# Fused bucketed attention and channel-mix kernel: transfers planned by DMA bandwidth, the second pair of heads turned by PE, v of four pairs left whole, and an early warm-up

## The chip, the cores and the metric

The kernel runs on one core of one Trainium2 chip. The metric is the device time of one execution in microseconds (us), lower is better. The profile's span (first to last instruction of the core) is about 2 us shorter than the time. An execution over 1.5% above the fastest of the same kernel counts as slow; ratios use the fast ones. A ratio is the mean time of one kernel's fast runs over that of the other's fast runs of the same rounds, so it is not quite the ratio of the medians that are quoted.

## The reference, cut to what matters

Attention in which a query sees only keys that fall in the same bucket (signs of six projections), then a channel mix on its result. The sizes are 4 batches, 8 heads, 768 positions, head dimension 64, model dimension 512, hidden dimension 1024, in float32.

```python
q_bits = (einsum('bhsd,dk->bhsk', q, proj) > 0)          # the same for k
mask   = bucket(q)[..., :, None] == bucket(k)[..., None, :]
scores = where(mask, (q @ k.T) / sqrt(D), -1e9)
attn   = softmax(scores) @ v                              # sum + 1e-9 below
x      = heads side by side                               # (B, S, 512)
x_prev = x shifted by one position
xk, xr = mu_k*x + (1-mu_k)*x_prev,  mu_r*x + (1-mu_r)*x_prev
out    = sigmoid(xr @ w_r) * (relu(xk @ w_k)**2 @ w_v)
```

The profile's names: a *pair* is two heads of one batch, so there are 16 pairs, four to a batch. The channel mix of a batch (called MoE in the program) can start only when all four of its pairs are finished and mixed.

## The kernel before

The program holds a small planner. Every operation is added with an engine, an estimated duration, a priority and its dependencies. A list scheduler then simulates all engines and fixes the order of instructions on each engine before the launch. On the chip each engine runs its list in that order, so one late operand holds everything behind it on that engine.

```python
LAG = {"PE": 0.35, "ACT": 0.30, "DVE": 0.30, "POOL": 0.30, "SP": 2.2, "GQ": 2.5}
# SP: transfers issued by SyncE; GQ: transfers issued by POOL. A transfer is
# done "lag" us after it was issued, however many others are in flight.
```

The parts that the change touches (cuts marked):

```python
# the projection, queued on ACT behind two k loads
for e in range(2):
    add("ACT", 0.06, -8.0, lambda e=e: nc.scalar.dma_start(out=pj[e * D : (e + 1) * D, :], in_=proj), w=[("pj", e)], lag=2.2)

# ten weight loads, each reading 512 KB of float32, from 10 us on
add("GQ", 1.1, 0.6 + 0.25 * i, f_w, w=[...], at=10.0 + 2.0 * i, lag=4.0)

def add_v(n):        # centre v: three POOL sums, a mean by matmul, two DVE ops
    ...              # vt, vs; mean: ones x vs; va = v - mean
def add_prep(n):     # q and k of a pair: hi and lo half-precision parts ...
    ...
    add("DVE", DVE_C(768, 2), n - 1.7, hi, ...)
    add("DVE", DVE_C(768), n - 1.7, lo, ...)
    # ... turned by a DMA transpose, one for q and one for k
    add("SP", 0.5, n - 1.5, tr, ..., lag=4.5, name=f"tr{n}")
    ...              # bits by PE and DVE, then four row copies by DMA:
    add("SP", 0.35, n - 0.7 + 0.01 * i, row, r=[("bx", sx, 0), ("bx", sx, 1)], w=[("ab", side, sa, j)])

def add_scores(n):   # nine steps of 1024 columns: PE scores, ACT exponential
    ...
def add_mix(n):      # xk = df*mu + x, in two DVE operations; the same for xr
    ...
```

Only pair 0 was turned by PE; pairs 1 to 15 by DMA.

The softmax here doesn't subtract the row's maximum and nothing guards it: scores larger than these inputs give would overflow.

Of the kernel before, what the change touches and what calls it, by code (L numbers as in the profile page):

```python
# [17 lines left out]
LAG = {"PE": 0.35, "ACT": 0.30, "DVE": 0.30, "POOL": 0.30, "SP": 2.2, "GQ": 2.5}  # L18
# [6 lines left out]
class Plan:  # L25
# [15 lines left out]
    def add(self, eng, dur, prio, fn, r=(), w=(), take=None, give=(), lag=None, name="", at=0.0):  # L41
        o = Op()
        o.i = len(self.ops)
        o.eng, o.dur, o.fn, o.prio, o.name = eng, dur, fn, prio, name
        o.take, o.give = take, give
        o.lag = LAG[eng] if lag is None else lag
        o.at = at
        deps = set()
        for key in r:
            if key in self.writer:  # L50
                deps.add(self.writer[key])
        for key in w:
            if key in self.writer:
                deps.add(self.writer[key])
            deps.update(self.readers.get(key, ()))
        for key in r:
            self.readers.setdefault(key, []).append(o.i)
        for key in w:
            self.writer[key] = o.i
            self.readers[key] = []  # L60
        o.deps = deps
        o.succ = []
        o.left = len(deps) + 1
        for d in deps:
            self.ops[d].succ.append(o.i)
        self.ops.append(o)
        return o

    def schedule(self):
# [17 lines left out]
        t = 0.0  # L87
        while len(order) < len(ops):
            while events and events[0][0] <= t + 1e-9:
                _, kind, i = heapq.heappop(events)  # L90
                if kind == 0:
                    met(i)
                elif kind == 1:
                    o = ops[i]
                    for s in o.succ:
                        if ops[s].eng == o.eng and o.eng not in ("SP", "GQ"):
                            met(s)
                else:
                    o = ops[i]
                    for s in o.succ:  # L100
                        if ops[s].eng != o.eng or o.eng in ("SP", "GQ"):
                            met(s)
                    for name in o.give:
                        cls, slot, moe = held.pop(name)
                        avail[cls].append(slot)
                        moe_held[cls] -= moe
            progress = False
            for e in free:
# [4 lines left out]
                while ready[e]:  # L113
                    item = heapq.heappop(ready[e])
                    o = ops[item[1]]
                    if o.take is not None:
                        cls, name, moe = o.take
                        if not avail[cls] or (moe and moe_held[cls] >= self.slots[cls][1]):
                            skipped.append(item)
                            continue  # L120
                    pick = o
# [15 lines left out]
                heapq.heappush(events, (t + o.dur, 1, o.i))  # L137
                heapq.heappush(events, (t + o.dur + o.lag, 2, o.i))
# [10 lines left out]
def kernel(  # L149
# [19 lines left out]
    P = 128  # L169
# [8 lines left out]

    QS = 4.0
# [12 lines left out]
    NQ, NNH, NAQ, NBX, NV, NVA, NPT, NOB, NRC = 3, 2, 3, 2, 3, 3, 2, 2, 4  # L192
# [6 lines left out]
    vt_t = [buf([P, 2, 3 * D], FP32, f"vt{i}") for i in range(1)]  # L199
    vs_t = [buf([P, 2, D], BF16, f"vs{i}") for i in range(NVS)]  # L200
    va_t = [buf([P, 2, NSC, D + 2], BF16, f"va{i}") for i in range(NVA)]
# [33 lines left out]
    ACT_C = lambda n: 0.093 + 0.833 * n / 1000.0  # L235
    MM = lambda n: n / 2400.0 + 0.0025
    POOL2 = lambda n: 0.08 + 2.2 * n / 1000.0


    def f_ids():  # L240
        nc.gpsimd.memset(idh, 0.0)
        nc.gpsimd.affine_select(
            out=idh, in_=idh, compare_op=ALU.not_equal, fill=1.0, base=0,
            pattern=[[-1, P]], channel_multiplier=1,
        )
# [5 lines left out]
    add("DVE", 0.08, -9.0, lambda: nc.vector.memset(p2, 0.0), w=["p2"])  # L251
    for i in range(NVA):
# [3 lines left out]
    for e in range(2):  # L256
        add("ACT", 0.06, -8.0, lambda e=e: nc.scalar.dma_start(out=pj[e * D : (e + 1) * D, :], in_=proj), w=[("pj", e)], lag=2.2)
# [6 lines left out]
    for t, src, key in ((muk, moe_mu_k, "muk"), (mur, moe_mu_r, "mur")):  # L264
# [3 lines left out]
        add("SP", 0.5, -0.5, f_mu, w=[key])  # L268
        add("DVE", 0.08, 0.5, lambda t=t: nc.vector.tensor_scalar(
# [4 lines left out]
    for i, (which, c0, n) in enumerate(wlist):  # L274
# [6 lines left out]
        add("GQ", 1.1, 0.6 + 0.25 * i, f_w, w=[("w" + which, c) for c in range(c0, c0 + n)], at=10.0 + 2.0 * i, lag=4.0)  # L281
# [4 lines left out]
    def add_load(n):  # L286
        b, t = divmod(n, NPB)
        s = n % NQ
        for side in "qk":
            if n == 0:  # L290
                for j in range(2):
                    def f(side=side, j=j):
# [3 lines left out]
                    add("SP" if side == "q" else "ACT", 0.4 if side == "q" else 0.06, -10.0 + j, f,  # L296
                        w=[("nat", side, s, j)], lag=2.6 + j * 0.5)
            else:
# [3 lines left out]
                add("SP", 0.4, n - 2.6, f, w=[("nat", side, s, j) for j in range(2)], lag=3.0)  # L302
# [4 lines left out]
        add("SP", 0.4, n - 2.3, fv, w=[("vn", n % NV)], lag=3.0)  # L307

    def add_v(n):
        s, sa, ss, sm_ = n % NV, n % NVA, n % NVS, n % NMC  # L310
        vn = vn_t[s].rearrange("p j (c d) -> p j c d", d=D)
        vt, vs = vt_t[0], vs_t[ss]

        def f1():
            nc.gpsimd.tensor_tensor(out=vt, in0=vn_t[s][:, :, 0 : 3 * D], in1=vn_t[s][:, :, 3 * D : 6 * D], op=ALU.add)  # L315

        def f2():
            nc.gpsimd.tensor_tensor(out=vt[:, :, 0:D], in0=vt[:, :, 0:D], in1=vt[:, :, D : 2 * D], op=ALU.add)

        def f3():  # L320
            nc.gpsimd.tensor_tensor(out=vs, in0=vt[:, :, 0:D], in1=vt[:, :, 2 * D : 3 * D], op=ALU.add)

        add("POOL", POOL2(384), n - 0.6, f1, r=[("vn", s)], w=["vt"], name=f"vsum{n}")
        add("POOL", POOL2(128), n - 0.6, f2, r=["vt"], w=["vt"])
        add("POOL", POOL2(128), n - 0.6, f3, r=["vt"], w=[("vs", ss)])
# [21 lines left out]
    def add_prep(n):  # L347
        s, sh, sa, sx = n % NQ, n % NNH, n % NAQ, n % NBX
        for side in "qk":
            nat, nh, a = side_nat[side][s], side_nh[side][sh], side_a[side][sa]  # L350
            def hi(side=side, nat=nat, nh=nh):
                nc.vector.tensor_scalar(out=nh[:, :, 0:D], in0=nat.rearrange("p j (c d) -> p (j c) d", d=D),
# [4 lines left out]
            def tr(side=side, nh=nh, a=a):  # L357
# [4 lines left out]
            add("DVE", DVE_C(768, 2), n - 1.7, hi, r=rn, w=[("nhh", side, sh)], name=f"hi{n}")  # L362
            add("DVE", DVE_C(768), n - 1.7, lo, r=rn + [("nhh", side, sh)], w=[("nhl", side, sh)], name=f"lo{n}")
            add("SP", 0.5, n - 1.5, tr, r=[("nhh", side, sh), ("nhl", side, sh)],
                w=ax + [("ab", side, sa, j) for j in range(2)], lag=4.5, name=f"tr{n}")
        for h in range(2):
# [16 lines left out]
            add("PE", 2 * MM(HALF) + 0.1, n - 0.8, f, r=["p1", "p2"] + [("a", side, sa, j) for side in "qk" for j in range(2)],  # L383
                w=[(nm,)], take=("sm", nm, 0), name=nm)
            add("DVE", DVE_C(HALF), n - 0.75, g, r=[(nm,)], w=[("bx", sx, h)], give=[nm], name=f"bx{n}")
        for i in (0, 1, 2, 3):
# [4 lines left out]
            add("SP", 0.35, n - 0.7 + 0.01 * i, row, r=[("bx", sx, 0), ("bx", sx, 1)], w=[("ab", side, sa, j)], name=f"row{n}")  # L391

    def add_prep_first(n):
        s, sh, sa = n % NQ, n % NNH, n % NAQ
        for j in range(2):
            pr = -8.0 + 2.0 * j
            for side in "qk":
# [17 lines left out]
                def ev(nm=nm, a=a, j=j, side=side):  # L415
                    i_ = sm(nm)[:, 0:HALF].bitcast(FP16)
                    if side == "q":
# [9 lines left out]
                add("DVE" if side == "q" else "ACT", DVE_C(768, 2) if side == "q" else ACT_C(768), pr, ev,  # L427
                    r=[(nm,)], w=[("a", side, sa, j), ("ab", side, sa, j)], give=[nm], name="ev" + nm)
            for side in "qk":
                for h in range(2):  # L430
# [6 lines left out]
                    def be(nm=nm, a=a, j=j, h=h):  # L437
# [3 lines left out]
                            scalar1=0x8000, scalar2=0x5400, op0=ALU.bitwise_and, op1=ALU.bitwise_or)  # L441
                    add("PE", 2 * MM(HALF) + 0.1, pr + 0.1, bits, r=["p1", "p2", ("a", side, sa, j)], w=[(nm,)], take=("sm", nm, 0), name=nm)
                    add("DVE", DVE_C(HALF), pr + 0.1, be, r=[(nm,)], w=[("ab", side, sa, j)], give=[nm], name="be" + nm)
# [31 lines left out]
    def add_pv(n):  # L475
        b, t = divmod(n, NPB)
        sp, sa, so = n % NPT, n % NVA, n % NOB
        for j in range(2):
# [3 lines left out]
            for g in range(3):  # L482
                def f(nm=nm, j=j, g=g):
                    oo = sm(nm)
                    for ic in (2 * g, 2 * g + 1):
                        for jc in range(NSC):
                            o = j * NSC * S + jc * S + ic * P
                            nc.tensor.matmul(oo[:, ic * 65 : ic * 65 + 65], pt_t[sp][:, o : o + P], va_t[sa][:, j, jc, 0 : D + 1],  # L488
                                             start=(ic == 0 and jc == 0), stop=(ic == NSC - 1 and jc == NSC - 1))
                add("PE", 12 * 0.0315, T + 0.02 * g, f, r=[("pt", sp, s) for s in steps] + [("va", sa, j), ("va1", sa)],  # L490
# [3 lines left out]
            def fd(nm=nm, sr=sr):  # L494
                oo = sm(nm)[:, 0:390].rearrange("p (c e) -> p c e", e=65)
                nc.vector.tensor_scalar(out=rc_t[sr][:, 0, :], in0=oo[:, :, D], scalar1=TINY, scalar2=None, op0=ALU.add)  # L496
# [6 lines left out]
            add("DVE", 2 * DVE_C(10), T + 0.1, fd, r=[(nm,)], w=[("rc", sr)], name=f"rc{n}")  # L503
# [9 lines left out]
        def fx(nm=nm):  # L513
            nc.vector.tensor_scalar(out=xt_t[sx][:, P:], in0=sm(nm)[:, 0:HALF].bitcast(BF16),  # L514
# [6 lines left out]
        add("DVE", DVE_C(768, 2) + 0.1, n + 1.45, fx, r=[(nm,), ("mc", smc)], w=[("xt", sx)], give=[nm], name=f"xt{n}")  # L521
        add("POOL", 0.25, n + 1.5, fs, r=[("xt", sx), ("xz", sx)], w=[("xs", sx)], name=f"xs{n}")

    def add_mix(n):
# [7 lines left out]
        for m, mu, dst in (("xk", muk, xk_t), ("xr", mur, xr_t)):  # L532
            def f1(mu=mu, dst=dst):
                nc.vector.tensor_scalar(out=dst[smx], in0=df_t[sd], scalar1=mu[:, t : t + 1], scalar2=None, op0=ALU.mult)

            def f2(dst=dst):
                nc.vector.tensor_tensor(out=dst[smx], in0=dst[smx], in1=x, op=ALU.add)
            pr = n + (1.65 if m == "xk" else 1.75)
            key = (m, smx)
            add("DVE", DVE_C(768, 4), pr, f1, r=[("df", sd), "mu" + m[1]], w=[key], name=f"{m}a{n}")  # L540
            add("DVE", DVE_C(768, 2), pr, f2, r=[key, ("xt", sx)], w=[key], name=f"{m}b{n}")

    def add_moe(b):
# [24 lines left out]
        for c in range(NSC):  # L568
# [28 lines left out]
            add("SP", 0.4, T + 0.35, st, r=[("os", so)], name=f"st{b}_{c}")  # L597
# [54 lines left out]
```

## Time and profile before

| | before |
|---|---|
| time, median of 3 | 289.43 us (288.86 to 290.68) |
| span of the profiled run | 290.1 us (its time 291.86 us, above the other three) |
| PE busy | 241.3 us (83%) |
| first exponential; first Relu of the channel mix | 18.1 us; 98.0 us |
| DMA share, 0 to 60 us | 1.03 of 16 engines |

First the page of the kernel before: its heading, and three rows of the second part, where the span is cut into 40 slices of 7.25 us and each digit is the busy share in tenths (for PEclk, the granted clock in tenths).

```profile
span 290.1 us, 6291 instructions
...
PE   0585412956968798999999999999999999999994
...
PEclk9999575895999999999999999999999999999998
DMA  7989999989387497374847370638270001111022
```

PE is often idle or half idle in the first 15 slices (109 us) and full after that. The early slices are also where DMA is full and where the granted clock falls to half. Busy times by stretch say it in numbers. The columns are: the stretch, its length, then busy us and instruction count of PE, PE weight loads, DVE, ACT and POOL, then clock, DMA share and GB/s. The two rows are the stretches that the prediction quotes.

```profile
17.00:113.00 96.00, 63.69 (x733) 37.05 (x732) 70.62 (x149) 56.34 (x65) 27.93 (x40) 0.86 0.90 195
113.00:286.00 173.00, 171.15 (x1703) 103.69 (x1720) 120.80 (x276) 123.36 (x168) 15.64 (x26) 1.00 0.40 99
```

```profile
0.00:60.00 60.00, 27.97 (x263) 15.70 (x264) 35.11 (x71) 20.14 (x22) 22.86 (x47) 0.83 1.03 221
60.00:110.00 50.00, 39.63 (x493) 23.56 (x491) 41.53 (x87) 37.39 (x44) 12.78 (x18) 0.93 0.75 194
110.00:290.00 180.00, 173.74 (x1719) 104.96 (x1733) 124.38 (x284) 126.09 (x173) 16.32 (x28) 1.00 0.39 98
```

The first 110 us are where time is lost: PE is busy 28.0 of 60, then 39.6 of 50 us. What PE waits for is in the chain of waits, the chain of work that ended last, followed back from the end. Each row has start, length and what filled it.

```profile
2.24 5.65 DMA pj<-in_proj_dram
...
21.52 10.16 DMA ak<-kh
...
32.51 5.68 DMA ak<-kh
...
42.30 6.71 DMA ak<-bx
...
60.82 4.32 DMA vn<-in_v_dram
...
80.99 3.79 DMA vn<-in_v_dram
```

The projection load (`pj`, 1.5 KB) opens the chain. Then come two DMA transposes (`ak<-kh` is k turned): 10.2 us and 5.7 us, where one at 99.6 us took 3.9 us. Then come the copies of pair 1's bucket bits into its turned tiles (`ak<-bx`). The bits were ready at 33.8 us, but SP issued these copies only from 41.3 us: in its list the rest of pair 2's transpose, one of pair 3 and three loads stand before them, and that one of pair 3 alone held SP for 4.4 us. So pair 1 waited for loaded transfers and for its place in SP's list. SP's timeline:

```profile
36.25 4.37 SPq L358 DMA_TRANSPOSE aq<-qh  x1
...
41.33 0.86 SPq L390 DMA_DIRECT2D aq<-bx  x1
```

From 60 us on, v loads are on the chain. ACT's timeline shows what pair 1's delay cost; in brackets is the idle time before the instruction and its releaser.

```profile
19.50 7.58 ACT L466 ACTIVATE pt<-sc 128x1024 bf16<-128x1024 f32 x8 [0.41 <-PE sc L462]
50.12 1.94 ACT L466 ACTIVATE pt<-sc 128x1024 bf16<-128x1024 f32 x2 [23.05 <-PE sc L462]
```

The first row ends pair 0 at 27 us; ACT then stands for 23 us.

### The profile page before, as it was taken

To read this page: it belongs to the slowest core of one execution; us is meant where nothing else is said; L and a number is where in the kernel's file an instruction comes from. 1 tells how busy PE (TensorE), PEld (TensorE's weight loads), DVE (VectorE), ACT (ScalarE), POOL (GpSimd) and SP (SyncE) were. 2 spreads that over 40 slices of the span, in tenths; PEclk is the share of its full clock that TensorE was granted. 3 is DMA by queue.
4 is the path that set the end of the run, shared out by engine and by line. 5 is a ranking of instruction groups with operands and counts; after the bars stand their busy time and mean duration, and the time that the engine had idled before them with its cause. 6 is when DMAs were issued, how large, how long until landed. Compare 5 with 4: busy or idle time off the path is not lost.

```text
span 290.1 us, 6291 instructions
## 1 busy us (share of the span) xinstructions
PE 241.3 (83%) x2470; PEld 144.2 (50%) x2488; DVE 201.0 (69%) x440; ACT 183.6 (63%) x237; POOL 52.0 (18%) x92
## 2 busy tenths in 40 slices
PE   0585412956968798999999999999999999999994
PEld 0333301531534565565656656565566666655441
DVE  0899440898697898979498989796677674476321
ACT  3247000873877787977677979676879887617420
POOL 2660324414231312300000303030200000000000
PEclk9999575895999999999999999999999999999998
DMA  7989999989387497374847370638270001111022
GB/s 228 314 197 153 263 199 215 236 180 278 82 233 161 130 252 161 79 187 129 210 146 161 99 145 29 129 114 187 92 129 23 4 7 50 61 72 40 28 82 107
DMA packets 67757, 40.55 MB, mean 140 GB/s; under 512 B 49960, under 2 KB 64144, under 8 KB 67728
## 3 DMA queue, kind: packets, MB, share of 16 engines
q1 hardware_dynamic: 65072, 37.14, 51.2%
q0 software_dynamic: 2208, 2.62, 6.4%
q8 instruction: 19, 0.31, 0.4%
q10 hardware_dynamic: 448, 0.40, 0.4%
q14 instruction: 10, 0.08, 0.1%
HBM read 24.12 MB, written 6.29 MB: 105 GB/s over the span
## 4 chain that ended last, share of the span: by engine, by line
PE 59%; DMA 17%; DVE 16%; POOL 2%; SPq 2%; issue 2%; ACTq 0%; ACT 0%; DVEq 0%; POOLq 0%
PE sc L462 14%; PE sm L585 13%; PE sm L556 10%; PE sm L488 8%; PE sm L575 6%; DMA ak<-kh 5%; DMA vn<-in_v_dram 4%; DMA ak<-bx 4%; PE sm L374 3%; DMA pj<-in_proj_dram 2%; PE sm L436 2%; DVE kh L355 1%; DMA aq<-qh 1%; PE sm L511 1%; SPq L358 1%
## 5 line engine op out<-in xcount | busy, mean ns | idle before, releaser
L466 ACT ACTIVATE pt<-sc 128x1024 bf16<-128x1024 f32 x144 | 143.5, 1028 | 63.7 <-PE sc L462 63.4
L462 PE MATMUL sc<-aq,ak 128*128 128x512 f16 (+1 forms) x384 | 86.4, 336 | 13.9 <-DMA ak<-bx 10.0
L462 PEld LDWEIGHTS <-ak 128*128 128x128 f16 x384 | 35.0, 99 | 44.8 <-issue 13.0
L556 PE MATMUL sm<-xk,wk 128*128 128x384 bf16 x256 | 48.4, 326 | 2.6 <-DVE ob L501 2.5
L488 PEld LDWEIGHTS <-pt 128*128 128x128 bf16 x1152 | 43.3, 98 | 10.5 <-issue 2.1
L585 PE MATMUL sm<-wv,k 128*128 128x512 bf16 x185 | 46.9, 379 | 0.5
L488 PE MATMUL sm<-va,pt 128*128 128x65 bf16 x1152 | 44.8, 195 | 0.7 <-DVE bx L378 0.7
L560 ACT ACTIVATE kr<-sm 128x384 bf16<-128x384 f32 x64 | 30.8, 496 | 8.7 <-PE sm L556 8.7
L556 PEld LDWEIGHTS <-wk 128*128 128x128 bf16 x256 | 24.0, 98 | 18.8 <-issue 4.4
L315 POOL TENSOR_TENSOR vt<-vn 128x384 f32<-128x384 f32 x16 | 18.3, 1141 | 78.5 <-DMA vn<-in_v_dram 78.5
L592 DVE SCALAR_TENSOR_TENSOR os<-rs,sm 128x512 f32<-128x512 f32 x24 | 16.4, 683 | 20.3 <-PE sm L585 19.2
L563 DVE TENSOR_TENSOR k<-kr 128x384 bf16<-128x384 bf16 x64 | 23.8, 383 | 7.1 <-ACT kr L560 7.0
L578 ACT ACTIVATE rs<-sm 128x512 f32<-128x512 f32 x24 | 14.4, 600 | 19.9 <-PE sm L575 15.2
L585 PEld LDWEIGHTS <-k 128*128 128x128 bf16 x192 | 18.1, 98 | 17.0
L518 POOL COPY xt<-xt 128x127 bf16<-128x127 bf16 x16 | 6.5, 408 | 103.9 <-DVE xt L514 103.9
L575 PE MATMUL sm<-wr,xr 128*128 128x512 bf16 x85 | 23.9, 379 | 0.5
L374 PE MATMUL sm<-ak,p 128*32 128x384 f16 x120 | 14.5, 354 | 7.3 <-DMA ak<-kh 7.3
L514 DVE TENSOR_SCALAR xt<-sm,mc 128x768 bf16<-128x768 bf16 x16 | 9.8, 612 | 15.2 <-PE sm L511 15.0
L496 DVE TENSOR_SCALAR rc<-sm 128x6 f32<-128x6 f32 x32 | 5.2, 162 | 20.6 <-PE sm L488 20.6
L378 DVE TENSOR_SCALAR bx<-sm 128x384 uint16<-128x384 uint16 x30 | 15.8, 549 | 5.2 <-PE sm L374 5.1
L501 DVE TENSOR_TENSOR ob<-sm,rc 128x384 bf16<-128x384 f32 x32 | 17.8, 557 | 1.1
L337 DVE SCALAR_TENSOR_TENSOR va<-sm,vn 128x384 bf16<-128x384 f32 x32 | 16.9, 549 | 0.8 <-PE sm L332 0.8
(58 smaller groups left out, 208.8 us busy)
## 6 DMA issues: line engine op xcount, KB each, us to landing
vn<-in_v_dram SPq DMA_DIRECT2D x16, 384.0 KB
out_dram<-os SPq DMA_DIRECT2D x24, 256.0 KB
qn<-in_q_dram SPq DMA_DIRECT2D x15, 384.0 KB
kn<-in_k_dram SPq DMA_DIRECT2D x15, 384.0 KB
wk<-in_moe_w_k_dram POOLq DMA_DIRECT2D x4, 256.0 KB, 7.2
wv<-in_moe_w_v_dram POOLq DMA_DIRECT2D x4, 256.0 KB, 5.3
wr<-in_moe_w_r_dram POOLq DMA_DIRECT2D x2, 256.0 KB, 7.7
aq<-bx SPq DMA_DIRECT2D x30, 9.0 KB
```

The costliest lines, as they stand in the source:

```text
L315: nc.gpsimd.tensor_tensor(out=vt, in0=vn_t[s][:, :, 0 : 3 * D], in1=vn_t[s][:, :, 3 * D : 6 * D], op=ALU.add)
L337: nc.vector.scalar_tensor_tensor(out=va_t[sa][:, j, :, 0:D], in0=sm(nm)[:, j * D : (j + 1) * D].unsqueeze(1).to_broadcast([P, NSC, D]), sc ...
L374: nc.tensor.matmul(ps[32 * i : 32 * i + 32, 0:HALF], w_, a[:, i // 2, h * HALF : (h + 1) * HALF], start=st, stop=not st)
L462: nc.tensor.matmul(ps[:, lo - s * STEP : hi - s * STEP], side_a["k"][sa][:, j, jc * P : (jc + 1) * P], side_a["q"][sa][:, j, q0 : q0 + hi ...
L466: nc.scalar.activation(out=pt_t[sp][:, s * STEP : (s + 1) * STEP], in_=sc_t[plan.slot[nm]], func=AF.Exp, bias=EBIAS, scale=ESC)
L488: nc.tensor.matmul(oo[:, ic * 65 : ic * 65 + 65], pt_t[sp][:, o : o + P], va_t[sa][:, j, jc, 0 : D + 1], start=(ic == 0 and jc == 0), stop ...
L501: nc.vector.tensor_tensor(out=ob_t[so][:, :, j * D : (j + 1) * D], in0=oo[:, :, 0:D], in1=rc_t[sr][:, 1, :].unsqueeze(2).to_broadcast([P, ...
L556: nc.tensor.matmul(ps[:, 0:HALF], wk_sb[:, d, fc * P : (fc + 1) * P], xk_t[mx[d]][:, h * HALF : (h + 1) * HALF], start=(d == 0), stop=(d = ...
L560: nc.scalar.activation(out=kr_t[sk], in_=sm(nm)[:, 0:HALF], func=AF.Relu, scale=0.5 ** 0.5)
L563: nc.vector.tensor_tensor(out=k2_t[s2][:, h * HALF : (h + 1) * HALF], in0=kr_t[sk], in1=kr_t[sk], op=ALU.mult)
L575: nc.tensor.matmul(sm(nr), xr_t[mx[d]][:, c * P : (c + 1) * P], wr_sb[:, d, :], start=(d == 0), stop=(d == NDC - 1))
L585: nc.tensor.matmul(sm(nv), k2_t[(b * NFC + fc) % NK2][:, c * P : (c + 1) * P], wv_sb[:, fc, :], start=(fc == 0), stop=(fc == NFC - 1))
```

## The change

The intent: let the planner know that transfers share a bandwidth, so that its order is one that the chip can keep, and take work off DMA and DVE in the first four pairs. The new limit (`BACKLOG`) acts only inside the plan: what the chip sees of it is another order in each engine's list. The core of the diff:

```diff
-LAG = {"PE": 0.35, "ACT": 0.30, "DVE": 0.30, "POOL": 0.30, "SP": 2.2, "GQ": 2.5}
+LAG = {"PE": 0.30, "ACT": 0.25, "DVE": 0.20, "POOL": 0.20, "SP": 1.8, "GQ": 2.0}
+BACKLOG = 1.5
 ...
+                    if o.svc > 0.3 and dma_free - t > BACKLOG:     # hold it back
+                        skipped.append(item)
+                        heapq.heappush(events, (dma_free - BACKLOG, 3, o.i))
+                        continue
 ...
+                if o.svc:                                          # one shared DMA server
+                    dma_free = max(t + o.dur + 0.9, dma_free) + o.svc
+                    lag = max(lag, dma_free + 0.6 - t - o.dur)
 ...
+    NWARM = 8
+    NPET = 1          # pairs up to this one are turned by PE
+    NUC = 4           # pairs whose v stays whole
+    POOL_HI = (1, 2)  # pairs whose hi is computed by POOL
-    NQ, NNH, NAQ, ... = 3, 2, 3, ...
+    NQ, NNH, NAQ, ... = 3, 2, 4, ...
 ...
+    for i in range(NWARM):   # dummy matmuls on zeros; an early Exp loads ACT's table
+        add("PE", 0.43, -20.0 + 0.1 * i, lambda: nc.tensor.matmul(sm("warm"), wz[:, 0:P], wz, ...), ...)
-        add("ACT", 0.06, -8.0, ... nc.scalar.dma_start(out=pj...), lag=2.2)
+        add("GQ", 0.6, -20.0, ... nc.gpsimd.dma_start(out=pj...), svc=0.05)
-        add("GQ", 1.1, 0.6 + 0.25 * i, f_w, ..., at=10.0 + 2.0 * i, lag=4.0)
+        add("GQ", 0.7, (2.2 + 0.5 * i) if which == "k" else (3.5 + 0.35 * i), f_w, ...,
+            at=(22.0 + 5 * i) if which == "k" else (34.0 + 3.5 * i), svc=1.5)
-            add("SP", 0.5, n - 1.5, tr, ..., lag=4.5)
+            if n <= NPET:    # 12 transposes a side by PE, two DVE copies a side
+                ...
+                continue
+            add("SP", 1.5, n - 1.8, tr, ..., svc=2.1)
+            # v of pairs 0 to 3: a POOL cast; the sum of v, times 1e-12, is added by one
+            # more matmul in PV, which also stands in for the mean of empty buckets
+                    if uc and g == 0:
+                        nc.tensor.matmul(oo..., tiny, vsu_t[n % NVS][:, j, :]... , start=True, stop=False)
-                nc.vector.tensor_scalar(out=dst[smx], in0=df_t[sd], scalar1=mu..., op0=ALU.mult)
-                nc.vector.tensor_tensor(out=dst[smx], in0=dst[smx], in1=x, op=ALU.add)
+                nc.vector.scalar_tensor_tensor(out=dst[smx], in0=df_t[sd], scalar=mu..., in1=x, op0=ALU.mult, op1=ALU.add)
```

Cut: some evictions of pair 0 moved from DVE to ACT, earlier priorities for preparing a pair, later loads of the mixing factors, and planned durations. Pairs 2 to 15 are still turned by DMA.

## The prediction

> **What bounds the kernel now.** The table of stretches shows two regimes. From 113 to 286 us PE is busy 171 of 173 us, clock 1.00, DMA share 0.40: bound by PE. From 17 to 113 us PE is busy 63.7 of 96 us, mean clock 0.86, DMA share 0.90: it waits.
>
> - The chain of waits opens with the projection load, 5.65 us, queued on ACT behind other loads; DVE idles 7.1 us for it (waits view). First scores: 17.4 us.
> - Pair 1's DMA transposes (10.2, then 5.7 us) and row copies (6.7 us) stand in the chain from 21.5 to 49 us. ACT idles 23 us between pairs 0 and 1, PE idles from 40 to 48 us, the clock falls to 0.5.
> - From 60 to 97 us attention takes 10 to 12 us a pair, though nine exponentials need 9.25 us (1028 ns each); v loads, POOL sums and DVE are on the chain.
>
> The MoE needs four finished pairs: its first Relu is at 98 us.
>
> **What the change does.**
>
> - Start: projection first on POOL's queue, early table load, PE warm-up. The Trainium skill, "Trainium Kernel Development and Optimization", Key Constraints, says that SP, ACT and POOL transfers share 16 DMA engines and interleave; the trace agrees (1.5 KB took 5.65 us at DMA share 0.75). The first k half had landed by 4.2 us: DVE can start 4 us earlier. Eight bit matmuls took 2.72 us, four later ones 0.9: warm-up saves 1 to 2 us. First scores at 11 us.
> - Pair 1 by PE: 24 transposes (six took 0.5 us) and four 0.55 us copies replace 16 us of DMA wait. The ACT gap shrinks to 2 to 5 us (DVE work, row copies).
> - DMA planning, weights after 22 us, a fourth transpose buffer: transposes at 20 to 60 us land in about 4 us (3.94 at 99.6), not 5 to 10.
> - Whole v, pairs 0 to 3: removes two 0.55 us and three 0.16 us DVE ops a pair, and takes sums and mean off the chain. Adds one 390-column matmul a head (estimated 0.16 us) and a POOL copy. "hi" of pairs 1 and 2 moves to POOL. DVE drops from about 9.5 to 8.5 us a pair; ACT sets the pace.
> - Mixing: one fused op for two (0.9 us), costed like "lo", 0.96: no gain.
>
> **On the critical path.** PE's dense work is about 228 us: 173 after 113, plus before that six pairs at 7.6 us and most of the first product. The change only starts it earlier. With scores from 11 us at 10 to 11 us a pair, four pairs are mixed by 60 us with 4.7 pairs' PE work (36 us) done. Then 192 us dense and a 4 us tail: 256.
>
> **Predicted: 256 us, 80% range 247 to 270.** Faster by over 2%: 0.95; within: 0.04; slower: 0.01.
>
> **Signs.** First exponential at 11 to 14 us; ACT gap before pair 1 under 6 us; first Relu at 56 to 66 us; PE over 97% busy from 65 us; clock not below 0.8 after 20 us; total PE busy within 8 us of 241; no v wait on the chain before 60 us; DVE busy down about 5 us.
>
> **What would make it wrong.** DMA is nearly full from 20 to 60 us (estimated 46 us of work for 40: 4.2 a pair in transposes, 3.5 in loads, 1.5 a weight load): 12 us a pair gives 265. SP issues in order, about 8.5 us a pair; a stall there repeats the gap. If ACT or DVE bursts break PE's density after an early start, 5 to 8 us come back.

The 4.2, 3.5 and 1.5 us of its DMA estimate are the planner's own service times in the diff (2.1, 1.15 and 1.5 us a transfer), not measurements. The 390-column matmul, estimated at 0.16 us, took 0.17 to 0.18 us from start to next start.

## The result, and the profile after

The time is 268.75 us (median of 4, 268.36 to 269.48), against 289.78 us of the kernel before in the same runs; ratio 0.9277, 95% interval 0.924 to 0.9314. It lies in the predicted range, but 12.75 us above the predicted 256.

| | before | after | predicted |
|---|---|---|---|
| time, us | 289.78 | 268.75 | 256 |
| first exponential, us | 18.1 | 16.5 | 11 to 14 |
| longest ACT wait before pair 1 ends, us | 23.1 | 2.8 | under 6 |
| four pairs' exponentials end, us | 86.5 | 59.4 | |
| first Relu, us | 98.0 | 69.1 | 56 to 66 |
| PE busy, 60 to 110 us | 39.6 of 50 | 44.0 of 50 | over 97% from 65 us |
| PE busy in all, us | 241.3 | 240.0 | within 8 |
| DVE busy in all, us | 201.0 | 193.3 | about 5 less |

The page after has the same shape with a shorter first part. The clock falls only once, in the second slice, and there is a hole in PE in the 13th, 14th and 16th slice (80 to 107 us; a slice is now 6.66 us).

```profile
span 266.3 us, 6293 instructions
...
PE   6597668878995897999999999999999999999994
...
PEclk9799999999999999999999999999999999999999
DMA  7953987769969667966949699768340011220132
```

The same stretches as before:

```profile
0.00:60.00 60.00, 45.14 (x526) 26.93 (x527) 44.40 (x75) 40.33 (x45) 34.85 (x57) 0.97 0.73 183
60.00:110.00 50.00, 44.02 (x460) 26.34 (x461) 40.07 (x83) 36.01 (x48) 11.60 (x17) 1.00 0.88 192
110.00:290.00 180.00, 150.81 (x1519) 90.83 (x1533) 108.83 (x229) 109.52 (x149) 18.60 (x31) 0.99 0.42 107
```

PE's work left after 110 us fell from 173.7 to 150.8, by 22.9 us, and the span fell by 23.8. (The profiled run of the kernel before was the slowest of its four, so about 2 us of the 23.8 are spread between runs.) So the gain is what the prediction named: not less PE work, but more of it done early. Pair 1's stall is gone from ACT's timeline:

```profile
24.41 3.77 ACT L521 ACTIVATE pt<-sc 128x1024 bf16<-128x1024 f32 x4 [0.21 <-PE sc L517]
...
33.52 2.85 ACT L521 ACTIVATE pt<-sc 128x1024 bf16<-128x1024 f32 x3 [2.82 <-PE sc L517]
```

The chain of waits after:

```profile
1.66 6.30 DMA qn<-in_q_dram
8.05 2.41 POOL qh L389
10.54 2.31 POOL kh L389
...
34.53 4.31 DMA ak<-bx
...
75.64 4.34 DMA vn<-in_v_dram
80.11 1.87 POOL vt L347
...
94.86 5.30 DMA vn<-in_v_dram
```

No transpose and no v load is on it before 60 us; one row copy of 4.3 us is (`ak<-bx`). Two things are new. It opens with q of pair 1 and two POOL operations of 2.3 us each (`qh` and `kh`, line 389), and from 75 us on it passes through v loads and POOL sums, at a time when PE was meant to be full. Three stretches of 8 us show that hole; the columns are as above.

```profile
64.00:72.00 8.00, 7.19 (x113) 4.89 (x113) 5.34 (x13) 6.38 (x9) 1.92 (x3) 1.00 1.21 222
...
80.00:88.00 8.00, 5.21 (x62) 3.26 (x60) 5.79 (x15) 6.24 (x8) 3.35 (x4) 1.00 1.14 250
...
96.00:104.00 8.00, 6.67 (x45) 3.19 (x43) 7.67 (x14) 6.60 (x8) 2.76 (x3) 1.00 0.68 204
```

In the first two DMA is over 1 (its packets overlap); in the second PE stands for 2.8 us, in the third for 1.3.

### The profile page after: what moved, and what is told of

Same layout as the page of the kernel before. It is cut to its first block, busy times and chain, and to the rows that moved or that the text cites. A ratio compares the mean times of both kernels' runs of the same rounds, so it can differ in the third digit from the quotient of the medians.

```text
span 266.3 us, 6293 instructions
## 1 busy us (share of the span) xinstructions
PE 240.0 (90%) x2501; PEld 144.1 (54%) x2520; DVE 193.3 (73%) x386; ACT 185.9 (70%) x241; POOL 65.1 (24%) x103
## 4 chain that ended last, share of the span: by engine, by line
PE 69%; DVE 11%; DMA 8%; POOL 4%; ACT 3%; issue 3%; SPq 1%; DVEq 0%; POOLq 0%; ACTq 0%
PE sc L517 17%; PE sm L645 14%; PE sm L616 13%; PE sm L547 11%; PE sm L635 7%; DMA vn<-in_v_dram 4%; PE sm L423 4%; ACT pt L521 3%; DMA qn<-in_q_dram 2%; DVE kh L392 2%; PE sm L573 2%; DVE qh L392 2%; DMA ak<-bx 2%; POOL vt L347 1%; DVE qh L389 1%
## 5 line engine op out<-in xcount | busy, mean ns | idle before, releaser
L517 PE MATMUL sc<-aq,ak 128*128 128x512 f16 (+1 forms) x384 | 82.2, 325 | 6.8 <-ACT pt L521 5.3
L517 PEld LDWEIGHTS <-ak 128*128 128x128 f16 x384 | 34.3, 97 | 32.8 <-issue 11.2
L616 PE MATMUL sm<-xk,wk 128*128 128x384 bf16 x256 | 47.6, 326 | 0.1
L347 POOL TENSOR_TENSOR vt<-vn 128x384 f32<-128x384 f32 x12 | 14.0, 1168 | 65.1 <-DMA vn<-in_v_dram 65.0
L652 DVE SCALAR_TENSOR_TENSOR os<-rs,sm 128x512 f32<-128x512 f32 x24 | 16.4, 682 | 17.9 <-PE sm L645 17.0
L623 DVE TENSOR_TENSOR k<-kr 128x384 bf16<-128x384 bf16 x64 | 22.9, 372 | 7.5 <-ACT kr L620 7.5
L638 ACT ACTIVATE rs<-sm 128x512 f32<-128x512 f32 x24 | 14.3, 598 | 19.9 <-PE sm L635 15.0
L583 POOL COPY xt<-xt 128x127 bf16<-128x127 bf16 x16 | 5.7, 359 | 89.8 <-DVE xt L579 76.4
L392 DVE SCALAR_TENSOR_TENSOR kh<-kn,kh 128x768 f16<-128x768 f32 x15 | 16.3, 1085 | 0.8 <-POOL kh L389 0.5
L392 DVE SCALAR_TENSOR_TENSOR qh<-qn,qh 128x768 f16<-128x768 f32 x15 | 16.7, 1113 | 0.1
L599 DVE SCALAR_TENSOR_TENSOR xk<-df,muk,xt 128x768 bf16<-128x768 bf16 x16 | 16.2, 1015 | 0.3
L599 DVE SCALAR_TENSOR_TENSOR xr<-df,mur,xt 128x768 bf16<-128x768 bf16 x16 | 16.3, 1023 | 0.0
```

What stands on the lines that cost most here:

```text
L347: nc.gpsimd.tensor_tensor(out=vt[:, :, :, 0:E], in0=src[:, :, 0:3, 0:E], in1=src[:, :, 3:6, 0:E], op=ALU.add)
L392: nc.vector.scalar_tensor_tensor(out=nh[:, :, D:P], in0=nat.rearrange("p j (c d) -> p (j c) d", d=D), scalar=QS, in1=nh[:, :, 0:D], op0=AL ...
L517: nc.tensor.matmul(ps[:, lo - s * STEP : hi - s * STEP], side_a["k"][sa][:, j, jc * P : (jc + 1) * P], side_a["q"][sa][:, j, q0 : q0 + hi ...
L599: nc.vector.scalar_tensor_tensor(out=dst[smx], in0=df_t[sd], scalar=mu[:, t : t + 1], in1=x, op0=ALU.mult, op1=ALU.add)
L616: nc.tensor.matmul(ps[:, 0:HALF], wk_sb[:, d, fc * P : (fc + 1) * P], xk_t[mx[d]][:, h * HALF : (h + 1) * HALF], start=(d == 0), stop=(d = ...
L623: nc.vector.tensor_tensor(out=k2_t[s2][:, h * HALF : (h + 1) * HALF], in0=kr_t[sk], in1=kr_t[sk], op=ALU.mult)
```

## The experiments

Every kernel gave a correct result. Ratios are to the kernel before, of the same rounds. The right columns are from the profiled run.

| run | median us | ratio (95% interval) | first Relu, us | PE work left at 110 us | span |
|---|---|---|---|---|---|
| the kernel before | 289.8 | 1 | 98.0 | 173.7 | 290.1 |
| before_pe_turn | 285.65 | 0.9863 (0.981 to 0.992) | 92.3 | 169.3 | 283.3 |
| no_backlog_limit | 278.75 | 0.9585 (0.951 to 0.966) | 86.6 | 163.2 | 277.5 |
| v_whole_everywhere | 272.62 | 0.9390 (0.935 to 0.943) | 70.8 | 155.7 | 270.7 |
| weights_early | 272.12 | 0.9360 (0.932 to 0.940) | 80.2 | 156.0 | 270.4 |
| v_centred | 271.37 | 0.9355 (0.931 to 0.940) | 73.8 | 155.7 | 270.6 |
| no_pe_turn | 270.77 | 0.9316 (0.926 to 0.937) | (slow) | | |
| proj_first | 270.63 | 0.9278 (0.920 to 0.935) | 76.1 | 155.1 | 269.6 |
| no_warm_up | 269.48 | 0.9250 (0.920 to 0.930) | 66.7 | 153.6 | 268.1 |
| the changed kernel | 268.75 | 0.9277 (0.924 to 0.931) | 69.1 | 150.8 | 266.3 |
| no_pool_hi | 267.97 | 0.9203 (0.915 to 0.925) | 68.9 | 151.7 | 266.2 |
| three_pairs_early_start | 261.34 | 0.9015 (0.898 to 0.905) | 65.6 | 144.2 | 259.4 |
| three_pairs_by_pe | 259.72 | 0.8922 (0.888 to 0.897) | 67.7 | 144.0 | 257.8 |

In every profiled row the span less the PE work left at 110 us is 113.8 to 116.4 us. This is 110 us plus the 3.8 to 6.4 us in which PE stands after 110 us; that these are so few is what is measured. PE is the limit there in all of these kernels, so what a part is worth is how much PE work it leaves; the first Relu alone does not tell it. Before 110 us busy time is no measure of work, since the clock differs: the run without the backlog limit was busy 84.6 us there at a clock of 0.86 and 0.93, the changed kernel 89.2 us at 0.97 and 1.00, yet it has 12.4 us more left. In three profiles (before, changed, three_pairs_early_start) 18 or 19 of the 288 matmul records of the last two products are missing, so their work left reads about 1 us low (an estimate: in the others PE is busy 10.0 of 10 us there, in these 9.9). Also planning_alone is told below; its profiled run was slow. Rounds ran on different chips, and differences under 1% between rows of different rounds are not resolved. And each edit, even of one constant, makes the planner place every operation anew, so a run shows a part together with the new order.

### Which part carries the gain

**before_pe_turn**: the kernel before with the PE turn of pair 1 alone.

```diff
+            if n <= 1:       # transposes by PE, copies by DVE, as in the change
+                ...
+                continue
             add("SP", 0.5, n - 1.5, tr, ..., lag=4.5)
```

> The kernel before, with one part of the change alone: pair 1 of q and k is transposed by PE and copied out of PSUM by DVE, instead of by two DMA transposes. Everything else, the order of the loads and the planner's constants too, is as before. Theory S (the gain is the stall of pair 1): the 23 us in which ACT waits between pairs 0 and 1 shrinks to under 8 us, and the time falls by 10 us or more, to about 278. Rival D (the gain is the planning of DMA traffic): with weights and loads still in the way, pairs 2 and 3 stall instead, and the time stays within 4 us of 289.8.

Measured: 285.65 us, 1.4% less. Pair 1 came 12 us earlier (37.8 instead of 50.1 us), and pair 2 stood instead. ACT's timeline of this run:

```profile
37.82 1.94 ACT L478 ACTIVATE pt<-sc 128x1024 bf16<-128x1024 f32 x2 [9.03 <-PE sc L474]
...
52.31 1.02 ACT L478 ACTIVATE pt<-sc 128x1024 bf16<-128x1024 f32 x1 [6.18 <-PE sc L474]
```

The first row is pair 1 after a wait of 9.0 us. The second is its last exponential, after 6.2 us more; pair 2 then starts at 56.6 us, after another 3.2. On this run's chain two v loads then take 8.1 and 7.2 us. The stall moved; most of it was given back.

**no_pe_turn**: the changed kernel without that part (`NPET = 0`).

> The changed kernel with NPET 0: pair 1 goes back to DMA transposes, all other parts stay. Theory S: pair 1 is late again, ACT waits 8 to 15 us before it, and the time rises by 6 to 12 us to 275 to 281. Rival D: planned traffic lets the two transposes land in 4 to 5 us each, the wait stays under 6 us, and the time rises by less than 3 us.

Measured: 270.77 us; by the ratios 0.4% more than the changed kernel, with intervals that overlap. With traffic planned, pair 1 by DMA is not late by more than about 3 us (the longest wait of ACT from 20 to 50 us, in the profiled run, which was a slow one). Removing the part that the prediction put second costs 1 to 2 us at most, which these runs do not resolve.

**no_backlog_limit**: `BACKLOG = 1e9`, all else as changed.

> The changed kernel with BACKLOG set to 1e9, so that the plan issues transfers as soon as their buffers are free; its DMA model and the late weights stay. Theory S: under 3 us of change. Rival D (the limit on what is in flight matters): transposes and v loads land later by several us in the first 60 us, and the time rises by over 5 us.

Measured: 278.75 us, 10 us more than the changed kernel. Its chain of waits:

```profile
22.79 4.76 DMA aq<-qh
...
52.76 9.40 DMA aq<-qh
...
74.99 6.95 DMA vn<-in_v_dram
```

Transposes (`aq<-qh`) take 4.8 to 9.4 us and a v load 7 us again. No other part costs as much when it is taken away: only the plan's limit on what is in flight went, and 43% (by the ratios) to 48% (by the medians) of the gain with it.

**planning_alone**: the planner, the late weights, the fourth buffer and the priorities kept, the other parts undone.

```diff
-    NPET = 1          +    NPET = 0
-    NUC = 4           +    NUC = 0
-    POOL_HI = (1, 2)  +    POOL_HI = ()
 # no warm-up matmuls, the projection on ACT, two mixing operations
```

> The changed kernel with only the planning kept (DMA bandwidth in the planner, limit on what is in flight, late weights, fourth buffer of the transposes, new priorities; the split of the first evictions stays too): pair 1 by DMA, v centred, hi on DVE, no warm-up matmuls, the projection on ACT, two mixing operations. Theory D, now ahead (the planning is most of the gain; the other parts are worth 2 to 3 us each): 272 to 278. If the parts are needed together (the planning gains only because the PE turn and the whole v take load off DMA and DVE): over 281.

Measured: 268.91 us once, and 273.49, 274.50 and 275.35 us, which count as slow beside it. Only the 1.5% rule separates them: the fast run and one of the slow ones had the same granted clock, 0.987. All four lie 15 to 21 us under the 290.0 of the kernel before. Planning alone is thus worth 15 us or more of the 21; how much more stays open. The fourth buffer, the new priorities and the moved evictions had no run of their own.

**weights_early**: the old release times and priorities of the weights under the new limit.

```diff
-  (2.2 + 0.5 * i) if which == "k" else (3.5 + 0.35 * i), ..., at=(22.0 + 5 * i) if which == "k" else (34.0 + 3.5 * i)
+  0.6 + 0.25 * i, ..., at=10.0 + 2.0 * i
```

> The changed kernel with the old release times and priorities of the ten weight loads (from 10 us on, 2 us apart) under the new limit. If the weights in the way of transposes and loads before 50 us are what the planning removed: 5 to 10 us more, 274 to 279, with waits for row copies or v before 60 us. If the limit on what is in flight is enough by itself: within 2 us of 268.8.

Measured: 272.12 us, 3.4 us more by the medians (0.9% by the ratios, just under what is resolved), between the two expectations. The first Relu came 11 us later (80.2), yet most was won back from 60 to 110 us, where the DMA share was 0.71 instead of 0.88; that the weights no longer stood in the way there fits, but was not tested. Its first two stretches, beside 45.1 and 44.0 us of PE in the changed kernel:

```profile
0.00:60.00 60.00, 41.48 (x439) 23.81 (x440) 38.06 (x67) 32.43 (x37) 34.40 (x57) 0.97 0.76 178
60.00:110.00 50.00, 47.49 (x556) 29.79 (x556) 41.34 (x85) 42.90 (x56) 11.77 (x15) 0.94 0.71 172
```

Moving the weights mostly moves a hole.

**v_centred**: `NUC = 0`.

> The changed kernel with NUC 0: v of the first four pairs is again centred through the POOL sums, a mean matmul and two DVE operations a pair; everything else stays. If the short v path is worth what the prediction says (1.5 us of DVE a pair, v off the chain before 60 us), the four pairs take 1 to 2 us each longer, the first Relu moves from 69 to 73 to 77 us, and the time rises by 4 to 8 us. If v was never what ended the wait, under 2 us.

Measured: 271.37 us, 2.6 us more by the medians (0.8% by the ratios), below the expected 4 to 8, and not resolved. The first Relu moved by 4.7 us, as expected.

**no_warm_up**: no dummy matmuls.

> The changed kernel without the eight warm-up matmuls. The prediction gave the warm-up 1 to 2 us at the start. In the changed kernel the granted clock still fell to 0.79 between 8 and 16 us, so I expect first scores within 1 us of the changed kernel's and a time within 1.5 us of 268.8; if the warm-up does what it is for, 1 to 3 us more.

Measured: 269.48 us, ratio 0.925 against 0.9277: no effect that these runs can show. The first exponential came at 15.7 us, even 0.8 us earlier than with them. The warm-up ends at 6.0 us, and after six transposes PE stands for 2.9 us behind DVE, which waits for the projection. The changed kernel's granted clock then was 0.50 from 11 to 14 us, just when PE was needed; without the warm-up it was 1.00 there. The Trainium skill, "TensorE: Matmul & The Clock Gate", Part 1, says that a busy window of about 3.4 us raises the clock and an idle one lowers it. The fall after the wait agrees in kind, though this wait is shorter than that window. (The trace of the changed kernel holds no clock record before about 7 us, where the profile writes 1.00; six warm-up matmuls took 2.74 us there, four of the same 512 columns later 0.86.)

### Where the missing 12.75 us are

**proj_first**: the projection at the head of the SP and ACT queues.

```diff
-        add("GQ", 0.6, -20.0, lambda e=e: nc.gpsimd.dma_start(out=pj..., in_=proj), ..., svc=0.05)
+        add(("SP", "ACT")[e], 0.42, -20.0, lambda e=e: (nc.sync, nc.scalar)[e].dma_start(out=pj..., in_=proj), ..., svc=0.05)
```

> The changed kernel with the two projection loads issued first of all on SP and ACT, ahead of q and k, instead of on POOL's queue. In the changed kernel the projection still landed at 7.9 us and DVE waited 2.9 us for it. If the queue order is what counts, it lands by 3 us, the first exponential comes at 12 to 14 us instead of 16.5, and the time falls by 2 to 5 us. If 24-byte rows are slow by themselves, it lands at 5 us or later and the gain is under 1.5 us.

Measured: 270.63 us, ratio 0.9278: nothing gained. The first exponential came at 18.5 us, 2 us later than in the changed kernel and not at 12 to 14. In the changed kernel the projection still landed at 7.9 us (DVE's timeline of the changed kernel):

```profile
7.92 0.17 DVE L279 TENSOR_SCALAR p<-pj 128x6 f16<-128x6 f32 x1 [2.88 <-DMA pj<-in_proj_dram]
```

In this run it landed at 3.0 us, so the order in which transfers are issued decided, and not the row size. (The queue changed too, but in the kernel before ACT's queue did not bring it sooner than 7.9 us.) But DVE then stood twice behind POOL (DVE's timeline of proj_first):

```profile
3.03 0.17 DVE L279 TENSOR_SCALAR p<-pj 128x6 f16<-128x6 f32 x1 [1.86 <-DMA pj<-in_proj_dram]
...
10.17 0.96 DVE L392 SCALAR_TENSOR_TENSOR qh<-qn,qh 128x768 f16<-128x768 f32 x1 [1.98 <-POOL qh L389]
13.15 0.96 DVE L392 SCALAR_TENSOR_TENSOR kh<-kn,kh 128x768 f16<-128x768 f32 x1 [2.02 <-POOL kh L389]
```

The planner gives `hi` on POOL 0.8 us. The groups of the changed kernel (line, engine, operation, tiles, count, then busy us and mean ns) have 2.2 to 2.3 us on POOL, against 0.66 us (k, shown) and 0.55 us (q) for the same operation on DVE before; the POOL fence comes first:

```profile
L389 POOL TENSOR_SCALAR qh<-qn 128x768 f16<-128x768 f32 x2 | 4.5, 2267 | 3.9 <-DMA qn<-in_q_dram 3.8
L389 POOL TENSOR_SCALAR kh<-kn 128x768 f16<-128x768 f32 x2 | 4.4, 2210 | 0.2
L341 POOL CAST va<-vn 128x768 bf16<-128x768 f32 x4 | 4.4, 1100 | 0.1
```

```profile
L352 DVE TENSOR_SCALAR kh<-kn 128x768 f16<-128x768 f32 x15 | 9.9, 659 | 0.3 <-DMA ak<-kh 0.2
```

**no_pool_hi**: `POOL_HI = ()`.

> The changed kernel with the hi operations of pairs 1 and 2 back on DVE. On POOL they took 2.2 to 2.4 us each (the planner has 0.8), and in the changed kernel DVE's in-order queue stood behind them before the first scores. If they caused the late start: first exponential at 13 to 14.5 us instead of 16.5, and 2 to 4 us less in time, 265 to 267. If the start is bound by the projection (7.9 us) alone, or the start is not what the end depends on: within 1.5 us of 268.8.

Measured: 267.97 us, 0.8% less by the ratios, with overlapping intervals; the first exponential came at 16.4 us, not earlier, since DVE still stood for the projection until 7.3 us. Two causes of the late start lie one behind the other, and each edit alone met the other.

**v_whole_everywhere**: `NUC = 16`.

> The changed kernel with NUC 16: every pair keeps v whole. Tells whether the waits for v and its sums between 75 and 103 us (4 us of PE idle) cost the time that my prediction lacked. If so: those PE waits for the POOL sums go away, 3 to 6 us less, about 264. If the missing time is the late start alone: within 2 us. The result may be less exact, since v is no longer centred before the rounding to bf16.

Measured: 272.62 us, 3.9 us more by the medians (1.2% by the ratios). PE no longer waits for the mean, but POOL's cast now waits for the same v loads (7.6 us the longest between 66 and 106 us), and pairs 5 and 6 start at 80.5 and 97.3 us, no sooner than with the sums (76.7 and 96.7). The sums on the chain were a follower; the load itself was late. The edit also gives PE more work: 24 more matmuls of 390 columns, 0.18 us each from start to next start (164.55 to 164.73 us), which is 4.3 us (an estimate), while twelve means of under 0.1 us go. PE was busy 244.7 us in all instead of 240.0, with the same 89 us before 110 us, so this work can account for most of the loss.

**three_pairs_by_pe**: `NPET = 3`, one constant.

> The changed kernel with NPET 3: pairs 1, 2 and 3 are turned by PE, so four more DMA transposes leave the full DMA stretch before 60 us. If DMA load is what still holds the pace of pairs 2 to 4 at 10 to 11 us: first Relu 3 to 6 us earlier than 69 us and a time of 261 to 266. If PSUM slots, DVE (8 copies of 0.55 us more) or the late start hold it: within 2 us of 268.8.

Measured: 259.72 us, better than expected; four of six runs were fast, at 257.98 to 259.82. By the ratios it is 3.8% under the changed kernel. The first Relu came only 1.4 us earlier, but PE has no hole after it:

```profile
0.00:60.00 60.00, 49.32 (x604) 30.40 (x605) 50.59 (x91) 41.78 (x47) 36.52 (x57) 0.97 0.78 191
60.00:110.00 50.00, 49.04 (x556) 30.78 (x553) 42.18 (x87) 42.45 (x56) 13.52 (x20) 1.00 0.85 179
110.00:290.00 180.00, 143.98 (x1416) 85.18 (x1413) 103.76 (x216) 101.39 (x140) 17.09 (x27) 1.00 0.38 99
```

PE does 4.2 us more before 60 us and 5.0 us more from 60 to 110 us; 6.8 us less is left after 110. The exponentials of pair 5 and pair 6 start at 68.5 and 81.2 us, instead of 76.7 and 96.7. Four DMA transposes fewer is all that was taken from the traffic, but the order changed with it. Run off the chip, the planner of each kernel.py shows that much of the hole was planned: the changed kernel's plan has pairs 5 and 6 start at 70.9 and 89.1 us, this one's at 61.9 and 74.4. So three parts of this gain were not told apart: bandwidth freed on the chip, a path for pairs 2 and 3 that does not pass SP's in-order queue, and a plan that no longer holds transfers back for those four transposes.

**three_pairs_early_start**: the same with `POOL_HI = ()` and the projection first.

> Three pairs turned by PE, and besides it hi of pairs 1 and 2 on DVE and the projection loads first on SP and ACT, the two edits that each alone gave nothing. Theory: each alone met the other's wait (with the projection first, DVE stood behind POOL's hi; with hi on DVE, it stood behind the projection at 7.3 us). Together the first exponential comes at 12 to 14.5 us instead of 17, and the time falls below the 259.7 of three pairs alone by 1 to 4 us, to 255 to 259. Rival: DVE, busy 31 of 32 us from 16 to 48 us with three pairs by PE, takes the 2.2 us of hi back, and the time stays at 259 to 262 whatever the start.

Measured: 261.34 us, 1% more than three pairs alone, with intervals that do not overlap: a miss. The first exponential did come at 14.3 us and the first Relu 2.1 us earlier, but from 60 to 110 us PE was busy 46.2 us instead of 49.0. The rival's time holds, though its reason is not shown: DVE was as busy from 16 to 48 us in both (31 of 32 us). Why the later stretch lost what the start won stays open, but the plan had it already: its planned end is 250.9 us, 1.6 us after that of three pairs alone (249.3), and the two spans differ by 1.6 us as well. The best kernel measured is three_pairs_by_pe.

### The planner's figure beside the chip's

The program's planner has its own estimate of the end. It is no measurement, but beside the span it shows what the change did:

| | planned end | span | slip |
|---|---|---|---|
| before | 251.7 | 290.1 | 38.4 |
| before_pe_turn | 249.0 | 283.3 | 34.3 |
| changed, no backlog limit | 257.3 | 277.5 | 20.2 |
| proj_first | 255.0 | 269.6 | 14.6 |
| v_whole_everywhere | 257.1 | 270.7 | 13.6 |
| v_centred | 259.2 | 270.6 | 11.4 |
| no_warm_up | 257.1 | 268.1 | 11.0 |
| changed, weights early | 261.2 | 270.4 | 9.2 |
| changed | 257.3 | 266.3 | 9.0 |
| no_pool_hi | 257.6 | 266.2 | 8.6 |
| three pairs by PE | 249.3 | 257.8 | 8.5 |
| three_pairs_early_start | 250.9 | 259.4 | 8.5 |

The planned ends come from running the planner of each kernel.py off the chip; the rows are all those with a fast profiled run. The changed plan is 5.6 us *longer* than the plan before. It is faster because the chip comes closer to keeping it: before, the first Relu was planned at 64.2 us and came at 98.0; after, planned at 63.4 and came at 69.1. The limit itself does not lengthen the plan, which ends at 257.3 us with and without it, but without it the slip is 11.2 us larger. Among the kernels that keep the limit the slip still runs from 8.5 to 14.6 us, so a plan ranks variants only roughly: that of proj_first is 2.3 us shorter than the changed one and its span 3.3 us longer.

## Why the prediction was right or wrong

- **Bound and mechanism: right.** PE's work stays (241.3 to 240.0 us) and is brought forward. The 240.0 include 3.8 us of warm-up matmuls. After 110 us PE stood only 3.8 to 6.4 us in every profiled fast run. The prediction's step "the change only starts it earlier" held, and so did its sign that the clock stays over 0.8 after 20 us (1.00).
- **Direction and size: right, near the upper end.** 268.75 us, in 247 to 270.
- **Pair 1's stall: right that it goes** (23.1 to 2.8 us), but the credit was mis-shared, and the 5.7 us transpose counted as pair 1's was pair 2's. The PE turn alone gave 1.4%; without it the changed kernel loses little. The plan's limit on transfers in flight is worth 9 to 10 us in this kernel, and planning alone some 15 or more of the 21.
- **First scores at 11 us: wrong.** The first exponential came at 16.5 us. I took it that reordering would free DVE at 4 us. The projection was only moved to another queue and landed at 7.9 us, as before; the sentence of "Trainium Kernel Development and Optimization", Key Constraints, that I quoted says just that, and I did not carry it through. POOL's `hi` at 2.2 to 2.3 us was not costed at all. Yet starting earlier did not shorten the whole: 14.3 us instead of 17.0 came with 1% more time.
- **Four pairs mixed by 60 us: mis-sized by 9 us.** The exponentials of four pairs ended at 59.4. They ran at 10.7 us a pair, within the predicted 10 to 11, but from a start that was 5.5 us late; the first Relu came another 9.7 us later, at 69.1.
- **The step that failed: "Then 192 us dense".** From the start of the channel mix PE was to be full; it was busy 44.0 of 50 us from 60 to 110 us, because pairs 5 and 6 came late: their first exponentials start 16.3 and 20.0 us after those of the pair before. The DMA share was 1.14 to 1.21 in two of the stretches shown, but the plan itself has 16.8 and 18.2 us there, so how much of it is the chip's bandwidth and how much the order is not shown. The prediction warned of ACT or DVE bursts with 5 to 8 us; that the size came near is luck, since the cause was another. With four transposes fewer, PE is busy 49.0 of those 50 us.
- **The account of the 12.75 us.** Predicted PE work left at 110 us: 252 − 110 = 142; measured 150.8, so 8.8 us. Time less span, which I left out: 268.36 − 266.3 = 2.1 us. Span less work left: 115.5 instead of 256 − 142 = 114, so 1.5 us (the missing records can have moved about 1 us from the 8.8 to here). Median less profiled run: 0.4 us. Three pairs by PE recovers 6.8 of the 8.8.
- **Whole v: right in kind, worth not resolved.** DVE fell by 7.7 us (5 predicted), 4.7 of it by whole v (v_centred has 198.0). No v load stood on the chain before 60 us, but none did in the kernel before either (the first at 60.8), so this sign tells nothing. By the medians it is worth 2.6 us; extending it to all pairs costs 3.9.
- **Warm-up worth 1 to 2 us: wrong.** Nothing was seen.
- **Fused mixing: right, no gain in DVE time** (it had no run of its own). One operation of 1.02 us stands for two of 0.46 and 0.57 us (for xr 0.41 and 0.56), in the groups of DVE, before and then after:

```profile
L537 DVE TENSOR_TENSOR xk<-xk,xt 128x768 bf16<-128x768 bf16 x16 | 9.1, 567 | 0.5
...
L534 DVE TENSOR_SCALAR xk<-df,muk 128x768 bf16<-128x768 bf16 x16 | 7.3, 456 | 0.4
```

```profile
L599 DVE SCALAR_TENSOR_TENSOR xk<-df,muk,xt 128x768 bf16<-128x768 bf16 x16 | 16.2, 1015 | 0.3
```

## What to carry to other kernels

Where engines run a fixed order, a schedule that ignores shared bandwidth is optimistic, and every late transfer then holds all that stands behind it; a plan with a cap on what is in flight can be the faster kernel, here without being a longer one. Freeing one stage only counts if the next stage's inputs come on time: look at the busy share of the limiting engine in the stretch after the one that you repaired. Where the order is made by a planner, look for a hole in the plan before you blame the chip. To judge many variants, find one number that the end follows (here the limiting engine's work left at a fixed time), since early milestones, such as a first score or a first Relu, moved without the time.

## What the Trainium skill lacked or had wrong

- "GPSIMD Engine Reference", section 4.1 (Engine selection), calls one-input operations on GPSIMD roughly line-rate. Here a multiply by a constant, float32 to float16, 128x768, took 2.21 to 2.27 us on POOL and 0.55 to 0.66 us on DVE, while a cast of the same size to bf16 on POOL took 1.10 us (spans on POOL are rough in these profiles). The page gives no measured time of a multiply by a constant.
- "VectorE: DVE Perf Modes", the perf-mode tier table, has no row for `scalar_tensor_tensor`. With bf16 tiles in SBUF, 128x768, it took 1.02 us, as much as a multiply and an add apart (0.41 to 0.46 and 0.56 to 0.57 us), so fusing gained nothing.
- "DMA: Bandwidth & Descriptors", section "DMA Transpose (X-bar)", has no landing time of a transpose in loaded queues (the page has only a bandwidth, under another heading). Here one took 3.9 us at a DMA share of 0.53 (96 to 104 us) and 9.4 to 10.2 us among other transfers.
- "Trainium Kernel Development and Optimization", Key Constraints (transfers of SP, ACT and POOL share the DMA engines), held: 1.5 KB landed at 7.9 us from ACT's queue and from POOL's, and at 3.0 us when it was issued first. The page does not say how long a small transfer waits behind larger ones.
